# Two tiles of phase one transposed by DMA instead of TensorE, in a fused attention and MLP kernel

## The chip, the cores and the metric

One core of a Trainium2 chip. The metric is the device time of one execution in microseconds (us). Executions of one kernel scatter by about 0.7 us around 1511 us, so a difference of a microsecond is at the limit of what the times can show. Where it matters I read the pieces from the profiles of single executions. The span is the time from the first to the last instruction of a profiled execution.

## The reference, cut to what matters

```python
xn = _layernorm(x)                       # x: 2048 tokens x 1024, bf16
return x + _A_ref(xn, ...) + _B_ref(xn, ...)

def _B_ref(x, w1, w2, w3, w4):
    h = _gelu(_layernorm(x) @ w1)        # phase one of the kernel: second norm, product with w1
    ...                                  # shifts of h, then @ w2: phase two
    x1 = x + hs
    return x1 + _gelu(_layernorm(x1) @ w3) @ w4
```

`_A_ref` is attention over 64 segments with a memory. In the kernel it takes the time after some 534 us; the change does not touch it.

## The kernel before

Phase one works on 16 tiles of 128 tokens. For each, VectorE makes statistics, the twice normalized tile `xn2` is formed and transposed into `xn2T`, and TensorE multiplies it with `w1`. Tiles 0 to 7 are normalized on VectorE and transposed on TensorE (a product with the identity into PSUM, the memory that takes TensorE's results, copied out by ScalarE: such a copy is called an eviction). Tiles 8 to 15 are normalized on ScalarE and transposed by a DMA issued from SyncE. The x tiles have ten buffers, so tile n+10 is loaded when the first norm of tile n has freed one.

```python
NPE = 8
def norm2(n, xn2T, jj):
    ...
    if n < NPE:
        ... nc.vector.tensor_scalar(xn2[:, c], xts[n][:, c], mv[:, 0:1], rr[:, 1:2], ...)
    else:
        nc.scalar.activation(xn2[:], xts[n][:], ACTF.Identity, bias=nm2[:], scale=rr[:, 1:2])
        nc.sync.dma_start_transpose(xn2T[:, jj], xn2[:])

def norm1(n):
    ...
    load_x(n + 10)

def transposes(xn2, xn2T, jj, half, halves=False):          # L293, L296
    ps = psum0.tile([P, 4, P], F32, tag="tr")
    for k in range(4):
        nc.tensor.matmul(ps[:, k, :], xn2[:, (half * 4 + k) * P:...], ident[:], start=True, stop=True)
    ... nc.scalar.copy(xn2T[:, jj, ...], ps[:, i:i + step])

def stage1(n0, nt, xn2T, between, j0=0):                    # L316: nt tiles times w1
    for co in range(KT):
        for k in range(KT):
            nc.tensor.matmul(ps[:, :w]..., w1_sb[:, k, co * P:(co + 1) * P], xn2T[:, j0:j0 + nt, k, :], ...)
        nc.scalar.activation(hTB[...], ps[:, :w], ACTF.Gelu_apprx_tanh)
        for f in between.get(co, ()):
            f()
...
for n0 in range(4, NT, 2):
    ...
    if n0 == 4:       # tiles 6 and 7 are transposed among the products of tiles 4 and 5
        for c in range(4):
            between[1 + 2 * c // 2 + (c > 1)] += [lambda c=c: tr(6 + c // 2, c % 2)]
    stage1(n0, 2, tiles2[n0], between)
```

At the very end the kernel stores the last output tiles (the last one on ScalarE's DMA queue, L719) and then reaches a branch (L883) to a fallback that is not taken here. A semaphore is a counter that a DMA raises when it has landed and that an engine can wait for. The framework gives the completion of the DMAs of SyncE and ScalarE to eight semaphores in rotation. On the way out SyncE waits for those eight, always in the same order; the instructions of the trace carry the semaphores' numbers, so the place of the last store in that order can be read.

## Time and profile before

| | before |
|---|---|
| time, median of 3 runs | 1511.2 us (1510.95 to 1512.2) |
| span of the profiled execution | 1509.3 us |
| TensorE busy | 1502.8 us |
| first transpose of tile 2 to first product of phase two | 53.09 us |
| issue of the last store to the end of the span | 3.40 us |

The prediction below shows the main lines. The chain in order of time gives the length of phase one, counted from the first transpose of tile 2, because what comes before it depends on when x and w1 arrive (columns: start, length, what):

```profile
15.33 0.22 PE ps L293 x4
...
68.42 6.69 PE ps L392 x31
```

L392 is the first product of phase two: 68.42-15.33 = 53.09 us.

### The profile page before, as it was taken

What the parts mean: (1) busy time and instruction counts of PE and PEld (TensorE: products, weight loads), DVE (VectorE), ACT (ScalarE), POOL (GpSimd) and SP (SyncE); (2) the same over time, 40 slices, a digit from 0 to 9 for tenths busy, and PEclk for the clock granted to TensorE, in tenths of its full rate; (3) what the DMA queues carried; (4) which work ended last, traced back from release to release, by engine and by line L of the source; (5) the groups of instructions that cost most, each with busy time, mean ns of one, the idle gap of its engine ahead of it and who ended that gap; (6) DMA issues with size and microseconds to landing.
All of it is one profiled execution on the core that took longest, in us unless ns stands there. A gap on an engine that the chain in (4) does not pass through costs nothing.

```text
span 1509.3 us, 24345 instructions
## 1 busy us (share of the span) xinstructions
PE 1502.8 (100%) x9850; PEld 804.6 (53%) x9850; DVE 545.0 (36%) x1136; ACT 504.6 (33%) x1144; POOL 175.4 (12%) x245
## 2 busy tenths in 40 slices
PE   9999999999999999999999999999999999999998
PEld 7844444445444444444456645664665455545555
DVE  8382230100020212222246624651564166516641
ACT  6533203013012011111156614650663266416630
POOL 5231020211111221100000000001000100010001
PEclk9999999999999999999999999999999999999999
DMA  8699762453345877622489957992998299918811
GB/s 296 147 273 314 222 174 88 143 202 106 133 152 150 200 243 257 218 98 81 129 225 251 241 128 168 258 246 67 236 256 202 73 227 222 219 60 204 212 48 51
DMA packets 303251, 272.41 MB, mean 180 GB/s; under 512 B 153894, under 2 KB 270152, under 8 KB 303136
## 3 DMA queue, kind: packets, MB, share of 16 engines
q1 hardware_dynamic: 281248, 189.92, 50.9%
q0 software_dynamic: 21744, 80.83, 15.6%
q8 instruction: 79, 1.29, 0.4%
q14 instruction: 36, 0.29, 0.1%
q10 hardware_dynamic: 144, 0.07, 0.0%
HBM read 190.08 MB, written 45.29 MB: 156 GB/s over the span
## 4 chain that ended last, share of the span: by engine, by line
PE 99%; DMA 1%; SPq 0%; DVE 0%; issue 0%
PE ps L654 30%; PE pso L712 15%; PE ps L593 15%; PE ps L534 13%; PE ps L560 13%; PE ps L392 4%; PE ps L316 3%; PE psS L669 2%; PE psO L693 2%; PE ps L852 1%; PE ps L484 1%; DMA w_sb<-in_B_w_dram 1%; PE gps L463 0%; PE ps L449 0%; PE ps L293 0%; SPq L234 0%
## 5 line engine op out<-in xcount | busy, mean ns | idle before, releaser
L654 PE MATMUL ps<-hTb,wt 128*128 128x396 bf16 (+2 forms) x2528 | 484.8, 342 | 0.0
L654 PEld LDWEIGHTS <-wt 128*128 128x128 bf16 x2528 | 236.8, 98 | 175.4
L593 PE MATMUL ps<-wt,xT 128*128 128x512 bf16 x1024 | 221.2, 379 | 0.0
L712 PE MATMUL pso<-wo_sb,oX 128*128 128x512 bf16 (+1 forms) x992 | 210.0, 372 | 0.0
L534 PE MATMUL ps<-xn3T,w_sb 128*128 128x512 bf16 x896 | 196.2, 379 | 0.0
L560 PE MATMUL ps<-w_sb,h3T 128*128 128x512 bf16 x896 | 195.5, 379 | 0.0
L593 PEld LDWEIGHTS <-xT 128*128 128x128 bf16 x1024 | 100.2, 98 | 120.8
L535 ACT ACTIVATE h3T<-ps 128x512 bf16<-128x512 f32 x112 | 66.9, 598 | 290.3 <-PE ps L534 289.4
L712 PEld LDWEIGHTS <-oX 128*128 128x128 bf16 x992 | 96.3, 98 | 107.4
L656 ACT CAST KT<-ps 128x462 bf16<-128x462 f32 (+2 forms) x160 | 81.8, 511 | 202.8 <-PE ps L654 198.7
L560 PEld LDWEIGHTS <-h3T 128*128 128x128 bf16 x896 | 87.0, 98 | 103.4
L534 PEld LDWEIGHTS <-w_sb 128*128 128x128 bf16 x896 | 86.6, 98 | 102.1
L675 DVE TENSOR_REDUCE sums<-sm 99x4 f32<-99x396 f32 (+2 forms) x176 | 97.6, 555 | 114.4 <-ACT sm L673 114.4
L658 ACT ACTIVATE QT<-ps 128x462 bf16<-128x462 f32 (+2 forms) x160 | 84.0, 525 | 120.2 <-PE ps L654 106.0
L595 ACT CAST Vs<-ps 128x512 bf16<-128x512 f32 x64 | 37.5, 586 | 233.2 <-PE ps L593 233.2
L671 DVE TENSOR_TENSOR sm<-psS,c_mask_reg_sb 99x396 f32<-99x396 f32 x152 | 86.7, 571 | 72.6 <-PE psS L669 72.5
L599 DVE CAST Vs<-ps 128x512 bf16<-128x512 f32 x64 | 44.3, 692 | 171.6 <-PE ps L593 171.6
L673 ACT ACTIVATE sm<-sm 99x396 f32<-99x396 f32 (+2 forms) x176 | 92.9, 528 | 34.5 <-DVE sm L671 27.6
L681 DVE TENSOR_TENSOR Pn<-sm,rs 99x396 bf16<-99x396 f32 (+2 forms) x176 | 98.9, 562 | 6.1 <-DMA PT<-Pn 0.2
L719 POOL DMA_DIRECT2D out_dram<-ot x30 | 16.4, 547 | 698.3 <-DVE ot L718 692.3
L561 DVE TENSOR_TENSOR R<-ps,R 128x512 f32<-128x512 f32 x32 | 21.9, 689 | 172.1 <-PE ps L560 155.3
L718 DVE TENSOR_TENSOR ot<-pso,Rt 128x512 bf16<-128x512 f32 (+1 forms) x33 | 22.3, 675 | 170.5 <-PE pso L712 166.5
(122 smaller groups left out, 1054.7 us busy)
## 6 DMA issues: line engine op xcount, KB each, us to landing
wt<-in_A_Wq_dram SPq DMA_DIRECT2D x76, 512.0 KB
wt<-in_A_Wk_dram SPq DMA_DIRECT2D x76, 512.0 KB
wt<-in_A_Wv_dram POOLq DMA_DIRECT2D x24, 1024.0 KB, 6.8
V_scratch<-Vs SPq DMA_DIRECT2D x32, 512.0 KB
V<-V_scratch SPq DMA_DIRECT2D x40, 384.0 KB
R_scratch<-x POOLq DMA_DIRECT2D x16, 512.0 KB, 4.1
R<-R_scratch SPq DMA_DIRECT2D x16, 512.0 KB
R_scratch<-R POOLq DMA_DIRECT2D x16, 512.0 KB, 3.1
```

Of the source, the lines that this page charges most:

```text
L534: nc.tensor.matmul(ps[:].rearrange("p (n t) -> p n t", t=P), w3_sb[:, k, f * P:(f + 1) * P], xn3T[tb][:, :, k, :], start=(k == 0), stop=(k ...
L535: nc.scalar.activation(h3T[:, f, :], ps[:], ACTF.Gelu_apprx_tanh)
L560: nc.tensor.matmul(ps[:], h3T[:, f, j * P:(j + 1) * P], w4_sb[:, f, ch * 512:(ch + 1) * 512], start=(f == 0), stop=(f == FT - 1))
L593: nc.tensor.matmul(ps[:], xT[:, m4 * 4 + j, k, :], wv[:, k, :], start=(k == 0), stop=(k == KT - 1))
L654: nc.tensor.matmul(ps[:, :nb], w[:, k, hh * P:(hh + 1) * P], B["hT"][:, k, :nb], start=(k == 0), stop=(k == KT - 1))
L656: nc.scalar.copy(dst[:, hh, :], ps[:, :nb])
L658: nc.scalar.mul(dst[:, hh, :], ps[:, :nb], scale)
L671: nc.vector.tensor_tensor(sm[:T, :, :T], S3, t["mask"][:].unsqueeze(1).to_broadcast((T, 4, T)), op=ALU.add)
L673: nc.scalar.activation(e[:T, :, :T], sm[:T, :, :T], ACTF.Exp, scale=LN2)
L675: nc.vector.tensor_reduce(ss, e[:T, :, :T], axis=AX.X, op=ALU.add)
L681: nc.vector.tensor_tensor(Pn[:T, :, :T], e[:T, :, :T], rs[:T, :].unsqueeze(2).to_broadcast((T, 4, T)), op=ALU.mult)
L712: nc.tensor.matmul(self.ps[:, :self.w], self.oX[0][:, h, self.oX[1] + self.gl * P:self.oX[1] + (self.gl + 1) * P], wo_sb[:, h, self.cc], s ...
```

## The change

The intent: take 16 transposes off TensorE, the engine that bounds the kernel, and let DMA do them. Tiles 6 and 7 keep their norm on VectorE. For the DMAs to be early enough their norms stand in the program before the end of the fourth tile's products, and the last three x loads are issued behind the two transposes.

```diff
-                    NPE = 8
+                    NPE = 6
...
-                        if n < NPE:
+                        if n < 8:
                             ... nc.vector.tensor_scalar(xn2 ...)
                         else:
                             nc.scalar.activation(xn2[:], ...)
+                        if n >= NPE:
                             nc.sync.dma_start_transpose(xn2T[:, jj], xn2[:])
...
-                        load_x(n + 10)
+                        if n < 3:
+                            load_x(n + 10)
...
-                    stage1(3, 1, tiles2[2], {0: [tr(4, 0)], 2: [tr(4, 1)], 4: [tr(5, 0)], 5: [tr(5, 1)]}, 1)
+                    def ahead(n):
+                        norm_stats(n + 1, 0)
+                        norm2_of(n)
+                        norm_stats(n + 1, 1)
+                        norm1(n - 2)
+
+                    stage1(3, 1, tiles2[2], {0: [tr(4, 0)], 2: [tr(4, 1), ahead(6)], 4: [tr(5, 0)], 5: [tr(5, 1), ahead(7)]}, 1)
+                    for n in range(13, NT):
+                        load_x(n)
...
-                        if n0 == 4:
-                            for c in range(4):
-                                between[1 + 2 * c // 2 + (c > 1)] += [lambda c=c: tr(6 + c // 2, c % 2)]
```

(The `lambda`s of the two `stage1` lines are left out here.)

More of the change, by code (lines that the diff above doesn't have):

```diff
@@ L265, in norm_stats @@
                         nc.gpsimd.tensor_tensor(rr[:], ab[:], neghalf[:], op=ALU.pow)
-                        if n >= NPE:
+                        if n >= 8:
                             nc.gpsimd.tensor_scalar(nm2[:], mv[:, 0:1], rr[:, 1:2], -1.0, op0=ALU.mult, op1=ALU.mult)
@@ L351 @@
                     load_consts(4)
-                    for n in range(1, NPE):
+                    for n in range(1, 6):
                         if n > 1:
@@ L362 @@
                             stage1(n - 1, 1, tiles2[(n - 1) // 2 * 2], {6 - n: [lambda n=n: tr(n, 0)], 7 - n: [lambda n=n: tr(n, 1)]}, (n - 1) % 2)
-                    stage1(3, 1, tiles2[2], {0: [lambda: tr(4, 0)], 2: [lambda: tr(4, 1)], 4: [lambda: tr(5, 0)], 5: [lambda: tr(5, 1)]}, 1)
+                    def ahead(n):
[3 more added lines that the diff above has]
+                        norm1(n - 2)
+                    stage1(3, 1, tiles2[2], {0: [lambda: tr(4, 0)], 2: [lambda: tr(4, 1), lambda: ahead(6)], 4: [lambda: tr(5, 0)], 5: [lambda: tr(5, 1), lambda: ahead(7)]}, 1)
+                    for n in range(13, NT):
+                        load_x(n)
                     def prep(n):
```

## The prediction

> **What bounds the kernel now.** I read the page first (busy time by engine, then the chain that ended last), then the chain in order of time around phase one, then the timelines of VectorE and of the SyncE queue there, then the DMA packets by stretches. The page:
>
> ```profile
> span 1509.3 us, 24345 instructions
> PE 1502.8 (100%) x9850; PEld 804.6 (53%) x9850; DVE 545.0 (36%) x1136; ACT 504.6 (33%) x1144; POOL 175.4 (12%) x245
> PE 99%; DMA 1%; SPq 0%; DVE 0%; issue 0%
> ```
>
> The reader is to see that TensorE is busy for 1502.8 of 1509.3 us and is 99% of the chain. Busy time by 50 us stretches leaves 2.5 us idle in the first stretch (x and w1 are still arriving) and none later, until the last product ends near 1505.4 us. So an instruction taken from TensorE after about 13 us shortens the run by its issue time, unless a wait takes its place, and what the other engines save is worth nothing by itself. The chain in order of time, asked for 20 to 75 us (start, length, what):
>
> ```profile
> 24.71 2.64 PE ps L316 x32
> 27.35 0.22 PE ps L293 x4
> 27.57 0.87 PE ps L316 x8
> 28.45 0.22 PE ps L293 x4
> 28.67 1.75 PE ps L316 x16
> 30.42 0.22 PE ps L293 x4
> 30.64 0.87 PE ps L316 x8
> 31.51 0.22 PE ps L293 x4
> 31.74 36.68 PE ps L316 x336
> ```
>
> L293 is a transpose of 128x128 as a product with the identity, L316 are the products with w1. These four pieces of four transposes each are tiles 6 and 7, standing among the products of tiles 4 and 5. Each delays the next product by 0.22 to 0.23 us. All four lie on the chain.
>
> **What the Trainium skill says.** (1) "TensorE: Matmul & The Clock Gate", section "Wait — 56ns, not 53.3ns?": a warm product with 128 columns starts 55.6 ns after the one before. The trace agrees: four transposes in 0.22 us are 55 ns each; the 219 ns that the groups show for one is its length with the pipeline, not its cost. (2) "VectorE: DVE Perf Modes", section "The three transpose paths": 390 ns for a 128x128 transpose on TensorE against 1309 ns by DMA. These are times to completion and would say "don't"; here the TensorE transposes are pipelined (eight blocks of a tile cost 0.45 us of issue), and one DMA instruction carries all eight blocks of a tile, so the figure that matters is whether it lands in time. (3) "DMA: Bandwidth & Descriptors", section "Queues, rings and completion order": each DMA engine takes descriptors in ring order within a queue and shares itself out among queues packet by packet. So a transpose stands behind the x and w2 loads issued earlier from SyncE and shares with the stores issued from GpSimd. The trace of before has no transpose in that congested stretch, so it cannot confirm this for a transpose. (4) Same page, "Rules for kernel authors": a transpose next to ordinary DMAs needs no ordering; all transposes stay on the one SyncE stream, so no serializing wait is added.
>
> **The change part by part.** *Removed on TensorE:* 2 tiles x 8 blocks = 16 transposes. From the chain, 27.57-27.35, 28.67-28.45, 30.64-30.42 and 31.74-31.51 are 0.22+0.22+0.22+0.23 = 0.89 us, all on the path.
>
> *Removed on ScalarE:* four PSUM evictions of 128x512 (L296, median 0.587 us), 2.35 us. ScalarE is busy 33% and holds no piece of the chain, so worth 0. It does move the first norms that ScalarE makes (tiles 8 and 9), but those also wait for GpSimd's small factors (tile 8's is ready at 29.61+0.27 = 29.88 us, and ScalarE began that norm at 29.91), so they hardly come earlier.
>
> *VectorE and GpSimd:* the instruction orders of the two builds show the same sequence there, tile by tile. So the norms of tiles 6 and 7 are ready when they were before. Timeline of VectorE (start, length):
>
> ```profile
> 24.12 0.55 DVE L274 TENSOR_SCALAR xn<-xt,mv,rr 128x1024 bf16<-128x1024 bf16 x1
> 26.83 0.55 DVE L274 TENSOR_SCALAR xn<-xt,mv,rr 128x1024 bf16<-128x1024 bf16 x1
> ```
>
> The first is tile 6 (ready at 24.67), the second tile 7 (ready at 27.38). "Among the fourth tile's products" is thus a place in the program; VectorE runs back to back through this stretch and sets the time.
>
> *Added:* two DMA transposes on SyncE. How long one takes, from the first one of before (tile 8):
>
> ```profile
> 31.18 1.36 SPq L277 DMA_TRANSPOSE xn2T<-xn  x1
> DMA packets 82, 0.26 MB, mean 220 GB/s; under 512 B 17, under 2 KB 17, under 8 KB 82
> DMA packets 1071, 0.32 MB, mean 270 GB/s; under 512 B 1056, under 2 KB 1056, under 8 KB 1071
> DMA packets 66, 0.21 MB, mean 149 GB/s; under 512 B 16, under 2 KB 16, under 8 KB 65
> ```
>
> The three packet lines are the stretches 31.2 to 32.4, 32.4 to 33.6 and 33.6 to 35.0 us. A tile of 256 KB goes as 1024 packets of 256 B, and the middle stretch holds them all: they start 1.2 us after the issue and are through 2.4 us after it. With an estimated 0.4 us for the signal I count 2.8 us from the start of the issue to the landing, in a quiet queue. The second one (tile 9, issued at 34.19) still has packets after 36.2, up to about 37.3, so 3 to 4 us is possible beside stores.
>
> Tile 7 is issued at about 27.4 and lands at 27.4+2.8 = 30.2, or near 31.4 with a slow one. Tile 6 is issued at 24.7, into a DMA system that is full: the share of the engines is 1.01 in 24.7 to 26.2 us, 0.59 in 26.2 to 27.7. It goes behind the loads of tiles 11 and 12, and I estimate its landing at 28 to 29. The products of tiles 6 and 7 begin now at 31.74 + 16 x 0.109 = 33.49 us (0.109 is 36.68/336); without the 0.89 us they begin at 32.6. The slack is 2.4 us for tile 7 by the quiet figure, 1.2 us by the slow one. So the DMAs should be hidden.
>
> *Moved:* the loads of x tiles 13 to 15. In before they are issued when the norm of three to five frees a buffer (about 23.5, 26.25 and 28.97 us). Now they stand behind the transpose of tile 7, so about 28.7, 29.1 and 29.5. At 2 to 3 us each they land by about 32.5. VectorE first reads tile 13 at 37.46 us. Slack 5 us, worth 0; it takes 0.75 MB out of the way of the two transposes.
>
> *Later waits:* one more pair of DMA semaphores is waited for before the products of tile 6 (in before, such an extra wait stands in the TensorE queue four times, 51 ns each, and TensorE shows no idle there), worth 0. ScalarE's norms of tiles 8 to 10 now wait for the transposes of 6 and 7 to have read their buffers. Tile 8's norm would be held only if tile 6 landed after 29.9, and TensorE only if ScalarE came another microsecond late, as four PSUM buffers lie between.
>
> **Sum:** -0.89 us on the path, everything else hidden: 1511.2 - 0.9 = 1510.3 us, a ratio of 0.9994.
>
> **The rivals.** *Rival 1, the wait takes the place of the transposes.* Tile 6 queues behind 2 MB of w2 and the x loads, and SyncE can issue tile 7 only after it. If tile 7 landed at 33.5 instead of 30.2 the gain would be gone, at 35 the run would be 1.5 us longer: 1511.2 to 1513. For it: the DMA share of 1.01 when tile 6 is issued, and a landing can slip by a microsecond. Against it: the share falls to 0.59 and 0.76 in the following stretches, 0.43 in 29.2 to 30.7, and the deferred x loads lighten it further. About 15%.
>
> *Rival 2, the gain is given back later.* A transfer that starts at a fixed time (w3, w4) could hold the next stage, so that TensorE, 0.9 us early, waits. Then 1511.2. For it: loads are large in phases two and three. Against it: after the first w1 load, the chain has only TensorE pieces, at the changes of phase too, and most transfers are started by buffers that TensorE frees, so they move along. About 10%.
>
> *Rival 3, more is won than the transposes.* If switching between transposes and products cost more than the 0.89 us, or ScalarE's 2.35 us held products back, the gain could be 1.2 to 2 us: 1509.5. Against it: the pieces follow each other without a gap at 109 ns per product before and after. About 5%.
>
> **Range and chances.** The three runs of before lie between 1510.95 and 1512.2, a scatter of about 0.6 to either side, which is of the size of the gain. Rival 1 pulls the upper end to about 1511.8, rival 3 and the scatter the lower to 1509.4. Two per cent would be 30 us; nothing in this change reaches it, since the whole stretch of phase one that it touches lasts 10 us and a late DMA costs a few. Within 2%: 0.99; 0.005 on either side.
>
> **What would show it right or wrong.** Right: 16 fewer instructions of TensorE and of its weight loads at the transposing line (48, not 64), 14 evictions instead of 18, ten DMA transposes into xn2T instead of eight, the first two issued near 24.7 and 27.4 us; in the chain one unbroken run of products of 256 columns from about 25.5 us on; phase two's first product about 0.9 us before 68.42; the span near 1508.4. Wrong by rival 1: a wait of TensorE on the DMA of xn2T between 32 and 36 us, or products further apart than 109 ns there. Wrong by rival 2: phase two starts early, but a DMA piece appears in the chain at a later change of phase. Wrong by rival 3: a phase-two start earlier by more than 1.2 us.

## More of the kernel before

The timeline of the end shows the issue of the last store on ScalarE's queue (start, length):

```profile
1505.85 0.38 ACTq L719 DMA_DIRECT2D out_dram<-ot  x1
```

The view of the branch's line shows SyncE's eight waits (durations, then the starts of the first and the last):

```profile
L883 SPq EVENT_SEMAPHORE  x8: 17/17/17, 1503.0 to 1507.5; - x8
```

Of the eight waits, six were over before the last store was even issued; the trace has them at 1502.96 to 1503.92. The seventh is the one for the last store (both carry the number 117), and it ended at 1507.45.

## The result, and the profile after

| | before | after |
|---|---|---|
| median of 6 runs | 1511.63 us (1510.58 to 1512.41) | 1511.49 us (1510.95 to 1513.0) |
| span of the profiled execution | 1509.3 us | 1509.4 us |
| TensorE busy, products | 1502.8 us, 9850 | 1501.7 us, 9834 |
| first transpose of tile 2 to first product of phase two | 53.09 us | 52.19 us |
| issue of the last store to the end | 3.40 us | 4.24 us |

The ratio is 1.0001, 95% interval 0.9988 to 1.0014. A ratio here is the mean time of one kernel's fast runs over that of the other's of the same rounds, so not quite the ratio of the medians. The predicted 0.9994 and no gain at all both lie in that interval, so the times alone decide nothing. The page of the changed kernel:

```profile
span 1509.4 us, 24313 instructions
PE 1501.7 (99%) x9834; PEld 803.5 (53%) x9834; DVE 544.8 (36%) x1136; ACT 502.8 (33%) x1140; POOL 175.4 (12%) x245
```

TensorE has 16 products fewer and 1.1 us less busy time, and yet the span is not shorter. The chain in order of time (L295 is now the transposes, L318 the products with w1, L400 phase two):

```profile
15.02 0.22 PE ps L295 x4
...
24.18 0.22 PE ps L295 x4
24.40 42.81 PE ps L318 x400
67.21 7.99 PE ps L400 x37
```

The four pieces of tiles 6 and 7 are gone, and 400 products follow each other without a gap. Phase one takes 67.21-15.02 = 52.19 us, 0.90 less than in before. That is the predicted 0.89. The view of the tile xn2T confirms the counts (ten DMA transposes, 14 evictions) and shows a wait that was not in before:

```profile
L298 ACT CAST xn2T<-ps x14: 373/587/592, 7.0 to 24.4; 128x512 bf16<-128x512 f32 x10, 128x256 bf16<-128x256 f32 x4
L278 SPq DMA_TRANSPOSE xn2T<-xn x10: 1232/1359/2255, 24.4 to 52.2; - x10
...
  ACT xn L276: 0.5, 1
```

ScalarE waited 0.5 us for a transpose. The timeline of SyncE's queue and that of ScalarE show which:

```profile
24.41 4.94 SPq L278 DMA_TRANSPOSE xn2T<-xn  x2
29.40 1.53 SPq L234 DMA_DIRECT2D xt<-in_A_x_dram  x3
31.04 19.77 SPq L278 DMA_TRANSPOSE xn2T<-xn  x7
```

```profile
37.60 1.24 ACT L276 ACTIVATE xn<-xt,nm,rr 128x1024 bf16<-128x1024 bf16 x1 [0.53 <-DMA xn2T<-xn]
```

The second piece of the queue is the three deferred x loads. They now go out just ahead of tile 8's transpose at 31.04. The norm at 37.60 is tile 11's and needs the buffer that this transpose reads. The transpose's semaphore was complete at 37.44, 6.40 us after the issue. In before the same transpose took 2.85 us (31.18 to 34.03).

And the end of the program, the store's issue and SyncE's waits at the branch (now L891):

```profile
1505.17 0.38 ACTq L727 DMA_DIRECT2D out_dram<-ot  x1
```

```profile
L891 SPq EVENT_SEMAPHORE  x8: 17/17/17, 1506.8 to 1507.7; - x8
```

The last store goes out 0.68 us earlier than in before, but the span ends 0.16 us later (1509.41). All eight waits now come after the store has landed: the first one ends at 1506.77, and seven more follow it.

**Theory "lane".** Two DMAs more on SyncE move the last store on by two of the eight semaphores, from the seventh to the first in SyncE's order. So seven waits, not one, are still to be gone through when it has landed, and the end grows from 3.40 to 4.24 us. **Rival "scatter".** The end varies by chance. **Theory "slack"**, for phase one: the DMA transposes are hidden only as long as they have time to spare, and the moved loads took some from tiles 8 and 9. Its rivals: they are hidden anyway, or a DMA wait is a chance of one run.

### The profile page after: what moved, and what is told of

The parts are those of the page before. It is cut to its first block, busy times and chain, and to the rows that moved or that the text cites. A ratio compares the mean times of both kernels' runs of the same rounds, so it can differ in the third digit from the quotient of the medians.

```text
span 1509.4 us, 24313 instructions
## 1 busy us (share of the span) xinstructions
PE 1501.7 (99%) x9834; PEld 803.5 (53%) x9834; DVE 544.8 (36%) x1136; ACT 502.8 (33%) x1140; POOL 175.4 (12%) x245
## 4 chain that ended last, share of the span: by engine, by line
PE 98%; DMA 1%; SPq 0%; issue 0%; DVE 0%
PE ps L662 30%; PE pso L720 15%; PE ps L601 15%; PE ps L542 13%; PE ps L568 13%; PE ps L400 4%; PE ps L318 3%; PE psS L677 2%; PE psO L701 2%; PE ps L860 1%; PE ps L492 1%; DMA PT<-Pn 1%; DMA w_sb<-in_B_w_dram 1%; PE gps L471 0%; PE ps L457 0%; PE ps L295 0%
```

## The experiments

### The end of the program

**before_again** and **after_again** are the two kernels unchanged.

> The kernel before once more, unchanged, for the scatter and a second profile. Both theories: ratio 1.000 within the interval. Theory 'lane' (the end of the program is longer in the changed kernel because the signal of the last store is the first of eight that SyncE waits for in turn, and was the seventh before): from the issue of the last store to the end of the span 3.4 us again, as in the first profile of before (1505.85 to 1509.25), SyncE's last wait at the branch line about 0.1 us after the one that was blocked. Theory 'scatter' (the 0.8 us at the end are chance): this length varies by half a microsecond or more between the two profiles of one kernel. Phase two's first product near 68.4 us, within 0.4.

> The changed kernel once more. 'Lane': from the issue of the last store to the end 4.2 us again (1505.17 to 1509.41 in the first profile), seven more waits after the one that was blocked; phase one ends 0.9 us earlier than in before, counted from the first product of tile 2. 'Scatter': the end is nearer to 3.4 us this time. The wait of TensorE on the transposed probabilities at 797 us, which cost 0.5 us, is not there again if it was chance. Ratio 0.999 to 1.001.

**after_tiny7** and **before_tiny2** put seven tiny DMAs into the changed kernel and two into the kernel before:

```diff
                     for n in (NT - 2, NT - 1):
                         norm1(n)
+                    tiny = cpool.tile([1, 7 * 16], BF16, name="tiny")      # 2 in before_tiny2
+                    for i in range(7):
+                        nc.sync.dma_start(tiny[:, 16 * i:16 * i + 16], A_mem0[0][0:1, 0:16])
```

> The changed kernel with seven DMAs of 32 bytes more, issued from SyncE when its queue is idle after phase one. They do nothing but move the last store on by seven of the eight completion semaphores, so that its signal is the last in SyncE's turn. 'Lane': from the issue of the last store to the end 3.3 us, 0.9 us less than in the changed kernel; time 1510.6 us, ratio 0.9994. 'Scatter', or seven more waits being free: 4.2 us, ratio 1.000.

> The kernel before with two DMAs of 32 bytes more at the same place, as many as the change adds, but with all transposes of tiles 6 and 7 on TensorE. 'Lane': from the issue of the last store to the end 4.2 us, as in the changed kernel, 0.8 us more than in before; time 1512.4, ratio 1.0005; phase one as in before. 'Scatter': 3.4 us, ratio 1.000.

Measured, 5 runs each beside 9 of the kernel before (median 1511.32):

| run | median us | ratio, 95% interval | last store's place | issue of the last store to the end |
|---|---|---|---|---|
| before_again | 1511.11 | 0.9998 (0.9985 to 1.0012) | 7 | 3.40 us |
| after_again | 1511.12 | 1.0001 (0.9988 to 1.0015) | 1 | 4.23 us |
| after_tiny7 | 1510.69 | 0.9997 (0.9983 to 1.0010) | 8 | 3.31 us |
| before_tiny2 | 1512.13 | 1.0012 (0.9999 to 1.0026) | 1 | 4.20 us |

The same view of the branch's line, first for before_tiny2, then for after_tiny7:

```profile
L886 SPq EVENT_SEMAPHORE  x8: 17/17/17, 1507.9 to 1508.8; - x8
```

```profile
L894 SPq EVENT_SEMAPHORE  x8: 17/17/17, 1503.3 to 1507.4; - x8
```

With two idle DMAs the kernel before has all its waits at the end, as the changed kernel has; with seven the changed kernel is rid of them. The lengths repeat to 0.01 us between two profiles of one kernel and came out as expected from the place alone, so "scatter" falls. (before_tiny2 had one run of 1516.35, which its mean carries; its ratio is no measure of the 0.8 us.)

What does scatter is elsewhere. Until the first transpose of tile 2 the profiles of before, before_again, before_tiny2, after and after_again take 15.33, 14.95, 14.39, 15.02 and 14.17 us. From phase two's first product to the last product they take 1436.95, 1438.72, 1438.23, 1437.48 and 1437.93 us, with short waits of TensorE on the transposed probabilities in attention, of both kernels. These two stretches each vary by more than the whole effect. The wait at 797 us that the first profile of the changed kernel had (0.36 us) came again in after_again (0.50), against what I had expected if it was chance, and in after_third (0.38); it is in before_again (0.77) and before_tiny2 (0.50) too, so it does not need the change.

**after_tiny3** puts three tiny DMAs into the changed kernel, otherwise the same edit.

> The changed kernel with three tiny DMAs more: the last store's signal is the fourth of eight in SyncE's turn, with four waits after it. If each wait costs about 0.085 us and the pause of 0.41 us falls only where more than four are left: 3.65 us from the issue of the last store to the end. If the pause stays: 3.97 us.

One look, 1511.72 us: 3.60 us to the end, near the 3.65 expected. Now the lengths can be ordered by the waits left after the last store's: none 3.31 (after_tiny7), one 3.40 (before), four 3.60 (after_tiny3), five 3.71 (npe4, below), seven 3.85 (no_move, below). That is (3.85-3.31)/7 = 0.077 us per wait. The changed kernel and before_tiny2, with seven waits left, have 0.35 to 0.39 us more: the trace shows one pause between two waits, 1506.96 to 1507.37 in the changed kernel, where neighbours are 0.06 to 0.1 us apart. The pause is in the same place in all three profiles of the changed kernel and not among the waits of no_move, so it belongs to the build. all_pe (below) has one further on (1511.79 to 1512.54 between two later waits of SyncE, 0.29 us apart in before) and 3.88 us to the end, where I had expected 3.40. So about 0.45 of the 0.84 us is the six more waits, and the rest the pause. It costs something only where it falls after the last store's signal: best (below) has it at 1502.16 to 1502.56, before its last store is issued. Its cause stays open. Where it can be seen among the eight waits, the trace has a packet of 8 KB, of the kind "instruction" on queue 14, 0.61 to 0.64 us after its end, so a load of the program's own instructions is a candidate that no run tested.

### Phase one

**all_pe**: the kernel before, with tiles 8 to 15 transposed on TensorE as well (norms still on ScalarE), among the products before them.

```diff
-                    NPE = 8
+                    NPE = 16
...
-                            nc.sync.dma_start_transpose(xn2T[:, jj], xn2[:])
...
+                        elif n0 < NT - 2:
+                            for c in range(4):
+                                between[3 + c] += [lambda c=c, n0=n0: tr(n0 + 2 + c // 2, c % 2)]
```

> The kernel before with tiles 8 to 15 transposed on TensorE too, so no DMA transpose in phase one. Theory 'issue time' (each tile's eight transposes cost TensorE 0.445 us of the path and nothing else): from the first transpose of tile 2 to the first product of phase two 53.09 + 8 x 0.445 = 56.65 us, time 1511.4 + 3.6 = 1515.0 us, ratio 1.0024. Eight DMAs fewer leave the last store's signal at its old place, so the end stays 3.40 us. Rival (ScalarE, with two evictions of 0.59 us more per tile, becomes the bound, or the transposes wait for norms): more than 57.2 us. Rival (time does not follow TensorE's issue time): ratio 1.000.

Median 1514.6 us, ratio 1.0020 (1.0006 to 1.0033). The chain in order of time:

```profile
14.86 0.22 PE ps L292 x4
...
39.80 0.35 PE ps L292 x4
...
71.90 0.21 PE ps L394
```

Phase one lasts 71.90-14.86 = 57.04 us, 3.95 more than in before. Eight tiles at 0.445 us are 3.56; three of the sixteen added pieces took 0.35 instead of 0.22 us, which makes up the other 0.39. No wait of TensorE is shown. So the issue time of transposes goes into the time, neither ScalarE's evictions nor the norms bound it, and this one effect is large enough to be seen in the times.

**npe4**: the changed kernel with tiles 4 and 5 by DMA too.

```diff
-                    NPE = 6
+                    NPE = 4
...
-                    stage1(3, 1, tiles2[2], {0: [tr(4, 0)], 2: [tr(4, 1), ahead(6)], 4: [tr(5, 0)], 5: [tr(5, 1), ahead(7)]}, 1)
+                    stage1(3, 1, tiles2[2], {2: [ahead(6)], 5: [ahead(7)]}, 1)
```

> The changed kernel with tiles 4 and 5 transposed by DMA as well, in the full DMA queue. 'The DMA is hidden only with slack' (rival 1 of the prediction, moved to where the slack is gone): tile 5's norm is ready at 21.6 us, its transpose lands 3 to 5 us later, 24.6 to 27, and the products of tiles 4 and 5 would begin at 24.0; TensorE waits 0.6 to 3 us on xn2T, against 0.89 us saved, so phase one from the first transpose of tile 2 lasts 51.9 to 54.3 us. 'DMA transposes are hidden anyway': 51.3 us. The end of the program is between 3.4 and 4.2 us, as the last store's signal is the third of eight.

Median 1521.79 us (1517.78 to 1523.15), ratio 1.0068 (1.0054 to 1.0082). The view of the waits, in 14 to 80 us (total, times, longest):

```profile
PE ps L318 <- DMA xn2T<-xn: 6.9, 1, 6.9
```

TensorE stood 6.9 us before the products of tiles 4 and 5, until 30.21 us. My expectation of 0.6 to 3 us had the right side and was far too small. The transpose of tile 5 was issued at 22.80 us and took 7.3 us to land; the eight of before took 2.7 to 7.1 us. The wait cost more than its length: the granted TensorE clock was 0.50 from 26.5 to 33.3 us, and the first 15 products after the wait started 0.213 us apart instead of 0.109, another 1.6 us. (The waits of 1.3 to 1.7 us in no_move, after_tiny3 and after_third left the clock at 1.00.) Phase one lasts 59.8 us, 6.7 more than in before. The profiled execution was the fastest of the five (1517.78); the other four are 2.8 to 5.4 us longer still, which no profile accounts for.

**no_move**: the changed kernel with the x loads in their old places.

```diff
-                        if n < 3:
-                            load_x(n + 10)
+                        load_x(n + 10)
...
-                    for n in range(13, NT):
-                        load_x(n)
```

> The changed kernel with the loads of x tiles 13 to 15 back in their old places, so 13 and 14 stand before the transposes of tiles 6 and 7. 'Slack': the transposes land up to 1 us later, by 32.2 us, still before the products of tiles 6 and 7 at about 32 us; phase one from the first transpose of tile 2 52.2 us as in the changed kernel, at most 0.3 more. 'The move is what made it work': TensorE waits on xn2T for 0.5 us or more, so 52.7 us or more. End 4.2 us in both.

Median 1512.15 us of 4 runs beside 1511.66 of before, ratio 1.0006 (0.9990 to 1.0021). The same view of the waits:

```profile
PE ps L317 <- DMA xn2T<-xn: 1.7, 1, 1.7
```

Here my own expectation ("slack") was wrong and its rival right: without the move, tile 7's transpose is late and TensorE waits 1.7 us, more than the 0.9 saved. Phase one lasts 54.04 us. The move is a needed part of the change, at least in this profile.

**after_third**: the changed kernel a third time, because after_tiny3 had shown TensorE waiting 1.6 us for tile 9's transpose, though its tiny DMAs come later than that.

> The changed kernel a third time. Four profiles have had its phase one (this kernel twice, and with three and seven tiny DMAs, which come only after it): three lasted 52.2 to 52.3 us from the first transpose of tile 2, one 54.0, with TensorE 1.6 us in wait for the transpose of tile 9. 'Slack': the transposes of tiles 8 and 9, now behind the loads of x tiles 13 to 15, land near 37.4 and 38.2 us for products at 39.3, so now and then one is late: this profile has either 52.2 us or a wait of 0.5 to 2 us on xn2T, and ScalarE waits on xn2T for the norm of tile 11. 'Chance of one run': 52.2 us, no wait of ScalarE on xn2T. End 4.23 us.

Median 1511.26 us beside 1510.65 of before, ratio 1.0002 (0.9988 to 1.0016). The chain:

```profile
32.74 6.81 DMA xn2T<-xn
39.56 0.14 issue
39.69 28.11 PE ps L318 x256
```

It happened again: the transpose issued at 32.74, tile 9's, lands 6.8 us later, and TensorE waits 1.3 us for it. Of five profiles with this phase one (the changed kernel three times, after_tiny3, after_tiny7) three last 52.19 to 52.28 us and two 53.62 and 53.98. None of the three profiles of the kernel before with or without tiny DMAs has a wait of that size (53.09, 53.09, 53.19), but the 53.19 is that of before_tiny2, where the first product of tile 8 came 0.11 us late, just after tile 9's transpose had landed (39.34 us). So tile 9 could be near the limit before the change too. ScalarE's wait on xn2T is in three of the five and neither in after_again nor in after_tiny7. The mean of the five is 52.85, so on this small count the gain of phase one is about 0.3 us on average, not 0.9.

### A version meant to repair both

**spread** issues the loads of x tiles 14 and 15 one transpose later each; **best** also loads w2 in three DMAs instead of four, which moves the last store from the first place to the eighth.

```diff
-                    for n in range(13, NT):
-                        load_x(n)
+                    load_x(13)
...
                     def prep(n):
                         norm2_of(n)
+                        if n in (8, 9):
+                            load_x(n + 6)
...
-                    for i in range(4):                                              # best only
-                        nc.sync.dma_start(w2_sb[:, 2 * i:2 * i + 2, :], w2_v[:, 2 * i:2 * i + 2, :])
+                    for a, b in ((0, 2), (2, 4), (4, 8)):
+                        nc.sync.dma_start(w2_sb[:, a:b, :], w2_v[:, a:b, :])
```

> The changed kernel with the loads of x tiles 14 and 15 each one transpose later (13 before the transpose of tile 8, 14 behind it, 15 behind that of tile 9). 'Slack': the transpose of tile 8 is no longer behind three loads, ScalarE does not wait on xn2T for the norm of tile 11, TensorE does not wait on xn2T; phase one 52.2 us. Rival: tiles 14 and 15 come too late for VectorE, and phase one is longer. End 3.85 or 4.23 us, as the last store's signal is the first of eight. Time 1510.8 to 1511.4.

> The same with w2 loaded in three DMAs instead of four, which makes the last store's signal the last of eight in SyncE's turn. 'Lane': 3.31 us from the issue of the last store to the end (3.7 if the pause of 0.4 us falls there), phase one 52.2 us; together 0.98 us less than before: 1510.4 us, ratio 0.9993. If ratio and end are as in the changed kernel, the turn of the signals was not the cause.

> The version with the spread loads and w2 in three DMAs once more. If both repairs are real and not chance: phase one from the first transpose of tile 2 52.2 us, no wait on xn2T, 3.3 us from the issue of the last store to the end, ratio about 0.9993 (0.9986 to 1.0000). If the first result was a lucky set of runs: ratio 1.000 with a wait on xn2T in the profile.

| run | median us | before beside it | ratio, 95% interval | phase one | last store to the end |
|---|---|---|---|---|---|
| spread | 1510.72 | 1510.65 | 0.9999 (0.9986 to 1.0013) | 52.19 us | 4.24 us |
| best | 1509.77 (1509.04 to 1510.38) | 1510.65 | 0.9992 (0.9978 to 1.0005) | 52.19 us | 3.29 us |
| best_again | 1510.03 (1509.71 to 1510.46) | 1511.14 | 0.9993 (0.9980 to 1.0007) | 52.20 us | 3.28 us |

The chain of best and its waits at the branch:

```profile
24.09 42.81 PE ps L318 x400
66.90 0.22 PE ps L401
```

```profile
L892 SPq EVENT_SEMAPHORE  x8: 17/17/17, 1501.9 to 1506.4; - x8
```

The 400 products run without a gap, as in the good profiles of the changed kernel, and seven of eight waits are over before the last store is issued. In all three profiles neither ScalarE nor TensorE waits on xn2T, and tile 8's transpose lands 2.92 to 3.18 us after its issue, against 4.55 to 6.98 in the five profiles with the three loads in front of it: that repair is shown. For tile 9 it is not: its transpose took 3.85 to 5.24 us here and 4.55 to 7.50 in the five, these overlap, and two of the five had no wait on xn2T either. The two ratios agree with the expected 0.9993, though each interval still contains 1. What is certain is the two lengths in the profiles: 0.90 us less in phase one and 0.11 us less at the end than in before.

## Why the prediction was right or wrong

The time of 1511.49 us lies inside the range, and "within 2%" was never in doubt. The predicted gain of 0.9 us did not come, and the span near 1508.4 us was 1509.4. Step by step:

- **Removed on TensorE, 0.89 us on the path: right.** Measured 0.90 from the first transpose of tile 2 to phase two (53.09 against 52.19), and again in after_again. all_pe confirms it with the opposite sign, at four times the size.
- **VectorE, GpSimd and ScalarE worth nothing: right.** The norms were ready at the same places, and ScalarE's saved evictions changed nothing.
- **The DMAs of tiles 6 and 7 hidden: right, by the slow figure.** They were issued at 24.41 and 27.09, and their semaphores were complete at 29.22 and 31.17 us, 4.8 and 4.1 us after the issue. The products of tiles 6 and 7 began at 24.40 + 0.89 + 64 x 0.109 = 32.3. So the slack was about 1.1 us, near the 1.2 I had given for the slow case. The slow case itself was read too low: I had let tile 9's packets in before end at about 37.3, but its semaphore was complete at 38.41, 4.2 us after the issue, and tiles 13 and 15 took 5.6 and 7.1 us. For the quiet case the 0.4 us that I had estimated for the signal holds: tile 8's packets in before were through by 33.6 us, and its semaphore was complete at 34.03. (That the 390 and 1309 ns of the skill are times to completion was my reading; the page does not say so.)
- **"Moved: slack 5 us, worth 0": wrong.** I asked only whether the x tiles would come in time for VectorE, which they did. I did not ask whom the moved loads would stand in front of: the transpose of tile 8. Its landing went from 2.85 us after the issue to 6.40, and spread, with two of the loads taken from in front of it, brings 2.96 back. The transpose of tile 9 is late in two of five profiles, at 1.3 and 1.6 us of TensorE's time; there the moved loads are a likely cause and not a shown one, as the change also brings tile 9's products 0.9 us nearer. The move also was not optional: no_move waits 1.7 us.
- **"Sum: everything else hidden": wrong, and this is where the gain of the first profile went.** The sum has no term for the end of the program. Two DMAs more moved the last store's signal to the first place in SyncE's turn, +0.84 us, which before_tiny2 brings back without any other part of the change and after_tiny7 takes away.
- **Rival 2, the gain given back later, at 10%: its outcome came, its mechanism did not.** I had looked for a weight load holding a phase. The chain indeed has only TensorE pieces at the changes of phase; what gave the gain back lies after the last product, where the chain no longer looks.
- **Rival 1 at 15%** named the right danger for the wrong tiles: not 6 and 7 but 9, and only now and then.
- **Rival 3 at 5%: not shown.** Phase two began 1.21 us earlier on the clock of the span (68.42 against 67.21), just past the 1.2 I had set as its sign. But 0.31 of that lies before the first transpose of tile 2, where the arrival of x and w1 decides; the stretch that the change touches gave 0.90.

Put together for the first profile: -0.90 in phase one and +0.84 at the end, so nothing beyond the scatter of the other stretches. With the average of five profiles in phase one, -0.3 + 0.84 = +0.6 us, a ratio of 1.0004, which the three measured ratios of the changed kernel (1.0001, 1.0001, 1.0002) neither show nor exclude.

## What to carry to other kernels

When work is moved from a bound engine to DMA, find out what the new transfers, and every load that is moved for them, now stand in front of, and read the slack from transfers in a full queue, not a quiet one. When a gain of a microsecond does not arrive, lay the two traces side by side at fixed marks, the last store and the end of the span among them: a change in the number of DMAs can alter how the program ends. At this size the pieces of the profile decide, because the times scatter by as much as the effect.

## What the Trainium skill lacked or had wrong

- No page says that a program's exit can depend on how many DMAs it has issued. "Runtime: NRT & Kernel Launch", section "The ~15µs preamble/postamble breakdown", gives about 1.5 us for the wait for all engines at the end, a barrier of the runtime after the kernel, and nothing on waits that the kernel itself ends with. Here the time from the issue of the last store to the end is 3.28 to 4.24 us, and each wait left after the last store's signal costs 0.077 us.
- "Advanced Engine Details and Errata", section "X-Bar Transpose (TRN2)", has transposes as fast as ordinary DMAs, at 350 to 400 GB/s. This transpose of a 128x1024 tile in packets of 256 B did not reach that. In before, tile 8's transpose moved 0.26 MB in 1.2 us with the engines 97% busy on it, 223 GB/s of engine time (0.26/1.2/0.97); the w2 load in 18.0 to 19.2 us moved 0.47 MB at 106%, 369 GB/s. Landing took 2.85 us for tile 8 in before and 6.40 us behind three loads in the changed kernel. The skill also has a lower figure for transposes of another layout, with which no run here compares.
